# Each part of the folded weights loaded as two transfers, its blocks on SP's queue and its sums on ScalarE's

## The chip, the cores and the metric

The kernel runs on one core of a Trainium2 chip. The metric is the device time of one execution, in microseconds (us), as the median of several executions. The core's engines are named as in the profile: PE (TensorE; PEld is its weight load), DVE (VectorE), ACT (ScalarE), POOL (GpSimd) and SP (SyncE, which here only issues transfers). A transfer (DMA) is issued by SP or by ACT, in the order of that engine's own instructions.

## The reference

An attention without softmax is followed by a multiplicative feed-forward block, all in float32:

```python
kv  = einsum('bhsd,bhse->bhde', k, v)          # 8 batches, 8 heads, 576 tokens, head size 64
o   = einsum('bhsd,bhde->bhse', q, kv)
x   = o / sqrt(mean(o*o, axis=-1) + 1e-6) * g_norm     # then (B,H,S,D) -> (4608, 512)
out = ((x @ w1) * (x @ w2)) @ w3 @ w_out       # w1, w2: 512x1024, w3: 1024x1024, w_out: 1024x512
```

## The kernel before, in words

**Folding.** The product `w3 @ w_out` (1024 x 512, called `w3o`) is worked out once, in the first 85 us, and kept in `w3o_sb`. Each token then needs two stages: the gates, (x w1)(x w2), and the projection by `w3o`.

**Groups.** The 4608 tokens are worked on in nine groups T of 512. Eight groups are the first 512 tokens of a batch; group 8 collects the last 64 of all eight batches. The order is 0 to 6, 8, 7. While PE works on a group, the attention of the next batch is done in pieces that a callback, `between`, lets in between two products (lines 1110 to 1115).

**Gates.** `gates` (line 748) runs `winograd` (line 616) four times a group (p = 0 to 3): seven products instead of eight, each of 8 PE instructions, all at line 623. Two PSUM banks, `r1` and `r2`, take several products one after the other; before the next product may go on in a bank, ACT copies the bank out (`keep`, line 636: p1, p5, u2, u3; and line 758 for c21). So PE waits for ACT when a copy is late. The last of the seven, `product("a22", "t4", r1)` at line 655, needs the copy u3.

**Projection.** Group 0 uses `winograd` again (`project`). From group 1 on, `project_twice` (line 865) applies the same scheme twice: seven `products(n)` of 28 PE instructions each, all at line 900. `products(n)` reads a part of `w3o`: 1024 columns of blocks (b11, b12, b21, b22) and 768 columns of sums of blocks (t1, t2, t4), 128 rows of 1792 float32, or 896 KB. In each `products`, the order is a11 b11, a12 b21, a22 t4, s1 t1, s2 t2, s4 b22, s3 t3: the first read of a sum is the third pair, after 8 of the 28 PE instructions.

**Where the parts are.** There are seven such parts, and they do not fit on the chip beside everything else. In group 1, the generator `prepare_b` (line 801) works out the sums part by part on DVE (lines 819 to 822) and stores each part to the DRAM tile `w3o_l2` in two stores on SP: the blocks at line 823, the sums at line 826. Parts 0, 3, 4 and 5 have their blocks in `w3o_sb`, parts 1, 2 and 6 in `w3o_sums` (tiles named `raw`). An eighth part holds 1024 columns of plain blocks for the very last product.

**Streaming.** `load_b` (line 832) brings the parts back, 56 loads in all, into three buffers in turn (`streams`): two are halves of `w3o_sb`, one is a `raw` tile, memory that the stores of `prepare_b` have read from. The first three loads are made in group 1's gates: load 0 as soon as the last step of `prepare_b` has been issued (the fourth call of `between`, at p = 1), loads 1 and 2 at the next call (p = 2, between the copies u2 and u3). From then on `project_twice` makes one load after each product, into the buffer that the product has just read; it is wanted two products later.

**Order.** SP, POOL and PE issue in the order of the program text (line 1013). DVE does so in `project_twice` and in the gates of p = 3 just before it. ACT, and DVE elsewhere, are put in order by the framework's planner before the run, by its own estimate of when each operation's inputs are there. Once the order is set, an engine waits at an instruction whose input is late, and everything behind it waits too. An ACT transfer stands in ACT's order like any other instruction.

Of the kernel before, what the change touches and what calls it, by code (L numbers as in the profile page):

```python
# [21 lines left out]
def kernel(  # L22
# [32 lines left out]
    nc = tc.nc  # L55
# [634 lines left out]
    PART = 7 * 2 * P  # L690
# [139 lines left out]
    ALL_B = 7 * (NG - 1)  # L830

    def load_b():
        n = len(loaded_b)
        if n == ALL_B:
            return
        t = streams[n % len(streams)]

        part = {ALL_B - 2: 6, ALL_B - 1: 7}.get(n, n % 7)

        queue = nc.scalar if n % 7 in (3, 5) else nc.sync  # L840
        if n + 1 < ALL_B:
            queue.dma_start(out=t, in_=w3o_l2[part])
        else:
            t = t[:, 0:1024]
            queue.dma_start(out=t, in_=w3o_l2[part, :, 0:1024])
        loaded_b.append(t)

    inner = {}
# [16 lines left out]
    def project_twice(T, last, ahead):  # L865
# [94 lines left out]
        r1 = products(0)  # L960
        p1 = keep("p1", r1)
        load_b()
        sum_inner(2)
        for f in ahead:
            f()
        r2 = products(1)
        p5 = keep("p5", r2)
        load_b()
        sum_inner(3)
        products(2, r1)  # L970
        z = keep("u2", r1)
        load_b()
        sum_inner(4)
        products(3, r2)
# [35 lines left out]
    w3o_l2 = dram.tile([8, P, PART], FP32, name="w3o_l2")  # L1010
# [9 lines left out]
    with tc.manual_schedule(  # L1020
# [6 lines left out]
        for e in range(2):  # L1027
            nc.scalar.dma_start(
                out=g_row[:, e * D:(e + 1) * D], in_=g_norm.rearrange("(o d) -> o d", o=1)
# [156 lines left out]
```

## Time and profile before

| what | us |
|---|---|
| median of 6 executions | 768.95 |
| lowest and highest of them | 767.5, 770.59 |
| the profiled execution | 770.52 |
| its span, first to last instruction | 768.7 |
| PE busy in the span | 760.2 (99%) |
| DVE, ACT, POOL busy | 541.2, 253.7, 134.8 |

The profiled execution is 1.57 us slower than the median, and 1.8 us of it lie outside the span. In the profile, an engine's "idle before" says how long it stood still before an instruction and what ended that; a line such as `SPq L842` is SP issuing the transfer written at line 842. Issues of transfers are not counted as busy time of the engine that issues them, so ACT's 253.7 us leave them out. Times within the span are counted from its start.

The 56 loads appear as four rows of issues at line 842 and one at line 845: 39 of 896 KB on SP, 16 of 896 KB on ACT, and one of 512 KB on SP.

### The profile page before, as it was taken

The numbers are of one execution on the slowest core, as the hardware profiler recorded it, in microseconds if no ns is written. First come the engines' busy times: TensorE is split into PE (matmuls) and PEld (weight loads), VectorE is DVE, ScalarE is ACT, GpSimd is POOL, SyncE is SP. The second block draws the span as 40 slices with busy tenths as digits, with TensorE's granted clock in tenths as the row PEclk, the third lists the DMA queues.
The fourth block names the chain that finished last, engine by engine and source line by source line (L and its number), as shares of the span: only waits on it lengthen the run. The fifth ranks groups of instructions, "written<-read, shape, count | busy, mean of one in ns | idle before, by whom it ended". The sixth has DMA issues, their size and how long they took to land.

```text
span 768.7 us, 14426 instructions
## 1 busy us (share of the span) xinstructions
PE 760.2 (99%) x5775; PEld 660.2 (86%) x5775; DVE 541.2 (70%) x1083; ACT 253.7 (33%) x487; POOL 134.8 (18%) x132
## 2 busy tenths in 40 slices
PE   8999999999999999999999999999999999999998
PEld 6455788888899889988998899889888998898897
DVE  7977999438978577756776777557665864595467
ACT  6777753213322332223213321332133222222221
POOL 0000000122610451133114411340144000000000
PEclk9999999999999999999999999999999999999999
DMA  9996641338997844874487648734841470075015
GB/s 310 345 335 175 218 137 43 83 91 257 329 295 255 229 109 123 271 211 104 130 270 190 125 134 279 191 102 136 285 80 43 143 249 0 1 240 151 1 37 190
DMA packets 133159, 132.55 MB, mean 172 GB/s; under 512 B 76644, under 2 KB 121188, under 8 KB 133092
## 3 DMA queue, kind: packets, MB, share of 16 engines
q1 hardware_dynamic: 130640, 116.81, 51.8%
q10 hardware_dynamic: 2452, 14.81, 5.6%
q8 instruction: 46, 0.75, 0.4%
q14 instruction: 21, 0.17, 0.1%
HBM read 100.27 MB, written 16.38 MB: 152 GB/s over the span
## 4 chain that ended last, share of the span: by engine, by line
PE 94%; DMA 3%; DVE 2%; ACT 0%; issue 0%; SPq 0%; ACTq 0%; DVEq 0%
PE mm L623 60%; PE mm L900 19%; PE mm L602 7%; PE at L332 3%; PE at L415 2%; DMA raw<-in_moe_w_out_dram 1%; DMA w3o_sb<-w3o_l 1%; DMA raw<-w3o_l 1%; PE at L589 1%; PE at L351 1%; PE at L951 0%; DMA raw<-in_moe_w_dram 0%; PE at L448 0%; PE at L433 0%; DVE xc L666 0%; DVE raw L860 0%
## 5 line engine op out<-in xcount | busy, mean ns | idle before, releaser
L623 PE MATMUL mm<-xT,w_sb 128*128 128x256 f32 x768 | 176.2, 379 | 0.0
L623 PEld LDWEIGHTS mm<-xT,w_sb 128*128 128x128 f32 x768 | 145.5, 190 | 20.0 <-issue 0.5
L623 PE MATMUL mm<-xc,ws 128*128 128x256 f32 x576 | 130.3, 379 | 0.0
L623 PEld LDWEIGHTS mm<-xc,ws 128*128 128x128 f32 x576 | 109.3, 190 | 15.1 <-ACT p L636 0.2
L762 DVE TENSOR_TENSOR c<-mm,u 128x512 f32<-128x512 f32 x36 | 24.9, 690 | 108.3 <-PE mm L623 108.3
L636 ACT COPY u<-mm 128x512 f32<-128x512 f32 x74 | 43.3, 585 | 138.7 <-PE mm L623 128.0
L636 ACT COPY p<-mm 128x512 f32<-128x512 f32 x74 | 43.4, 586 | 84.1 <-PE mm L623 79.9
L623 PE MATMUL mm<-xc,w_sb 128*128 128x256 f32 x288 | 69.2, 383 | 0.0
L900 PE MATMUL mm<-w3o_sb,raw 128*128 128x128 f32 x500 | 62.5, 276 | 0.1
L602 PE MATMUL mm<-chunks,ab 128*128 128x512 f32 x128 | 60.2, 601 | 1.6 <-DVE chunks L170 0.8
L623 PE MATMUL mm<-xT,ws 128*128 128x256 f32 x256 | 61.2, 382 | 0.0
L763 DVE TENSOR_TENSOR ab<-c 128x256 f32<-128x256 f32 x108 | 59.0, 546 | 3.0
L290 POOL COPY xT<-xn 128x1024 uint16<-128x1024 uint16 x26 | 32.1, 1262 | 163.0 <-DVE xn L393 162.9
L623 PEld LDWEIGHTS mm<-xc,w_sb 128*128 128x128 f32 x288 | 53.7, 190 | 7.6
L900 PEld LDWEIGHTS mm<-w3o_sb,raw 128*128 128x128 f32 x500 | 59.0, 192 | 0.5 <-DVE raw L858 0.3
L623 PEld LDWEIGHTS mm<-xT,ws 128*128 128x128 f32 x256 | 47.9, 190 | 6.9 <-ACT p L636 0.3
L384 DVE TENSOR_REDUCE inv<-sq 128x8 f32<-128x512 f32 (+1 forms) x40 | 23.4, 626 | 36.4 <-ACT sq L383 36.4
L762 DVE TENSOR_TENSOR c<-p,u 128x512 f32<-128x512 f32 x36 | 28.2, 784 | 27.0 <-ACT u L636 26.9
L900 PE MATMUL mm<-w3o_sb,ab 128*128 128x128 f32 x336 | 43.9, 275 | 0.7 <-DMA w3o_sb<-w3o_l 0.7
L911 ACT COPY u<-mm 128x512 f32<-128x512 f32 x23 | 13.5, 586 | 87.6 <-DVE raw L924 60.3
L900 PEld LDWEIGHTS mm<-w3o_sb,ab 128*128 128x128 f32 x336 | 41.1, 192 | 1.2 <-issue 0.9
L602 PEld LDWEIGHTS mm<-chunks,ab 128*128 128x128 f32 x128 | 21.8, 190 | 22.6 <-issue 15.8
(158 smaller groups left out, 1138.4 us busy)
## 6 DMA issues: line engine op xcount, KB each, us to landing
w3o_sb<-w3o_l SPq DMA_DIRECT2D x26, 896.0 KB, 5.2
raw<-in_moe_w_dram SPq DMA_DIRECT2D x31, 512.0 KB, 7.2
raw<-w3o_l SPq DMA_DIRECT2D x13, 896.0 KB, 5.9
w3o_sb<-w3o_l ACTq DMA_DIRECT2D x11, 896.0 KB, 4.6
k_sb<-in_k_dram SPq DMA_DIRECT2D x32, 256.0 KB, 4.4
v_sb<-in_v_dram SPq DMA_DIRECT2D x32, 256.0 KB, 4.6
q_sb<-in_q_dram SPq DMA_DIRECT2D x32, 256.0 KB, 4.1
out_dram<-raw SPq DMA_DIRECT2D x14, 512.0 KB, 3.6
```

The source lines that it names most:

```text
L290: nc.gpsimd.tensor_copy(to, src.rearrange("p a n w -> p w a n"))
L332: nc.tensor.matmul(kv_ps[e * D:(e + 1) * D, r - rs[0], :], lhsT=k_sb[:, e, cols] if j < J else kl[:, 2 * r + e, :], rhs=v_sb[:, e, cols] i ...
L351: nc.tensor.transpose(qt_ps[:, e, i, :], q_sb[:, e, i * P:(i + 1) * P], ident)
L384: nc.vector.tensor_reduce(out=inv[:, i], in_=sq.rearrange("p (h d) -> p h d", d=D), axis=AX.X, op=ALU.add)
L415: nc.tensor.matmul(o_ps[l][tokens, n * D:(n + 1) * D], lhsT=qT[r][rows, e, i, tokens], rhs=kv_b[rows, e, r, :], start=True, stop=True,)
L602: nc.tensor.matmul(sums_ps[half][m], lhsT=w3T[half, c][:, m, :], rhs=chunks[:, c, 1, :], start=(c == 0), stop=(c == KF - 1),)
L623: nc.tensor.matmul(ps[:, u, :], lhsT=lhsT(a_name, u, c), rhs=rhs(b_name, c),  start=(u == 0 and c == 0 and to is None), stop=(c == chunks ...
L636: nc.scalar.copy(t, ps)
L762: nc.vector.tensor_add(c, one, two)
L763: nc.vector.tensor_mul(dst, c[:, 0, :], c[:, 1, :])
L900: nc.tensor.matmul(to[:, i, :], lhsT=x[:, c, :], rhs=y[:, c, :], start=new and place // 4 not in seen, stop=(c == 1), skip_group_check=True,)
L911: nc.scalar.copy(t[:, 0:4], ps[0])
```

## The change

Each load of a part becomes two transfers: the 1024 columns of blocks (512 KB) on SP's queue and the 768 columns of sums (384 KB) on ACT's queue. Until now a load was one transfer, on ACT's queue for loads 3 and 5 of every seven and on SP's queue for the others. The last load, of the eighth part, stays one transfer of 512 KB on SP's queue. The number of bytes, the buffers and the places of the calls of `load_b` are the same.

```diff
         part = {ALL_B - 2: 6, ALL_B - 1: 7}.get(n, n % 7)
 
-        queue = nc.scalar if n % 7 in (3, 5) else nc.sync
-        if n + 1 < ALL_B:
-            queue.dma_start(out=t, in_=w3o_l2[part])
-        else:
-            t = t[:, 0:1024]
-            queue.dma_start(out=t, in_=w3o_l2[part, :, 0:1024])
+        nc.sync.dma_start(out=t[:, 0:1024], in_=w3o_l2[part, :, 0:1024])
+        if part < 7:
+            nc.scalar.dma_start(out=t[:, 1024:PART], in_=w3o_l2[part, :, 1024:PART])
         loaded_b.append(t)
```

## The prediction

> **What bounds the kernel now.** I read the busy times first, then PE's rows in the projection stages, then the transfers, then ACT, SP and DVE in group 1.
>
> ```profile
> PE 760.2 (99%) x5775; PEld 660.2 (86%) x5775; DVE 541.2 (70%) x1083; ACT 253.7 (33%) x487; POOL 134.8 (18%) x132
> ```
>
> PE is busy for 99% of the span, so nothing can gain much; the question is where PE still stands still. The loads are read only in the projection stages. One of 196 instructions takes from its first L900 row to the first L623 row of the next group:
>
> ```profile
> 601.56 1.50 PE L900 MATMUL mm<-raw,ab 128*128 128x128 f32 x12
> ...
> 623.44 1.89 PE L623 MATMUL mm<-x_left,w_sb 128*128 128x256 f32 x8
> ```
>
> That is 21.88 us, or 0.112 per instruction and 3.13 per product. The stages that begin at 298.50, 373.95 and 450.21 take 21.88 too. Three take longer: 221.52 to 244.12 (22.60), 525.65 to 548.49 (22.84), 671.79 to 694.56 (22.77). The last two each hold one wait for a load:
>
> ```profile
> 545.29 1.57 PE L900 MATMUL mm<-w3o_sb,ab 128*128 128x128 f32 x12 [0.72 <-DMA w3o_sb<-w3o_l]
> 688.23 1.58 PE L900 MATMUL mm<-raw,ab 128*128 128x128 f32 x12 [0.65 <-DMA raw<-w3o_l]
> ```
>
> So late loads cost 0.96 + 0.89 = 1.85 us in this execution, and group 1's stage another 0.72, where PE waits for sums made by DVE (the chain of waits runs through DVE from 218 to 232.7). The whole that could be won from the loads is 1.85, with group 1's 2.57.
>
> **The transfers.** Issues at line 842 and 845, columns: how many, size, median us from issue to landing:
>
> ```profile
> w3o_sb<-w3o_l SPq DMA_DIRECT2D x26, 896.0 KB, 5.2
> w3o_sb<-w3o_l ACTq DMA_DIRECT2D x11, 896.0 KB, 4.6
> w3o_sb<-w3o_l SPq DMA_DIRECT2D x1, 512.0 KB, 3.5
> ```
>
> A load issued when product k has ended is wanted when k + 2 has: 2 x 3.13 less 0.2 for the issue, about 6.0 us. The medians fit in that; the two late ones landed after 6.8 and 6.7 us.
>
> **The change, part by part.**
>
> *Bytes and landing.* The two single-transfer rows, 512 KB in 3.5 and 896 KB in 4.6, give 1.1 us per 384 KB and so 2.0 us that do not depend on size. If the two halves of a load overlap, both land by about 4.6 as now; if one runs wholly after the other and pays the 2.0 again, the blocks land at 3.5 and the sums at 6.6. The sums are wanted 8 x 0.112 = 0.9 us after the blocks, at 6.9, so even then neither is late by itself. A load delayed by 2.2 us, as the two late ones were (6.8 against 4.6), would have blocks at 5.7 to 6.8: PE waits 0 to 0.8 instead of 0.9. I take a third of the 1.85 off, 0.6; the ends are 1.85 off and, if two more of the 32 urgent loads (four in each of eight stages) came late at 0.9 each, 1.8 on.
>
> The Trainium skill, page "DMA: Bandwidth & Descriptors", section "Rules for kernel authors", speaks against the split: issuing from several engines brings no bandwidth, since all share the same 16 DMA engines, and only saves issue time; it wants transfers of 1 MiB or more. Its fit of 2.0 us plus bytes / 436e3 (measured on another issuing path) would make 896 KB 4.1 us and the halves, one after the other, 6.1; by that the term would be the same.
>
> *Issues on SP.* 56 instead of 40, 16 more at 0.33 us (the L842 rows). They stand at loads 3 and 5 of a stage, where SP has nothing else: in the stage of 298.50 its last issue before ended at 292.6. In group 1 load 3 now comes behind SP's transposes, which end at 224.8; on ACT it went at 225.06. Nothing. The stores of results and the q, k, v loads behind load 9 are behind it already.
>
> *Issues on ACT.* 55 instead of 16, 39 more at 0.33, 12.8 us beside ACT's 33%. In the stages each stands after a product that has ended, or just before: for load 4 after p5's copy, 6 after product 3, when ACT's next row waits 6.60 us anyway; 7 after u3's copy, 8 after product 5, with ACT idle until 319.25 in that stage. Load 9 stands beside the last copy, and may push it by 0.33; the copy's results go to DVE, which then still has 1.5 us of rows of `finish(p1)` before it. Nothing in the stages; the end above is 0.33 for each of seven, 2.3.
>
> *PE's extra waits.* 55, one for each sums transfer. L900 has 82 such semaphore instructions of 51 ns now, nine of them in the stage at 298.50, which still takes 196 x 0.112. So 0; the end is 55 x 0.051 = 2.8.
>
> *The end of the program.* Load 54, 896 KB on ACT, becomes two; load 55 stays. Its product began without a wait; 0.
>
> *Group 1: three new waits in ACT's order.* Loads 0 to 2 were on SP alone. Their sums now stand in ACT's order, and they overwrite what the stores of `prepare_b` read. SP in group 1:
>
> ```profile
> 201.09 0.53 SPq L823 DMA_DIRECT2D w3o_l<-w3o_sb  x1
> 201.72 0.45 SPq L826 DMA_DIRECT2D w3o_l<-raw  x1
> 202.26 1.02 SPq L823 DMA_DIRECT2D w3o_l<-w3o_sb  x1
> 203.37 1.03 SPq L826 DMA_DIRECT2D w3o_l<-raw  x1
> 204.50 1.12 SPq L823 DMA_DIRECT2D w3o_l<-raw  x1
> 205.72 1.28 SPq L826 DMA_DIRECT2D w3o_l<-raw  x1
> 207.09 1.00 SPq L842 DMA_DIRECT2D w3o_sb<-w3o_l  x1
> ```
>
> The three L823 rows are the blocks of parts 4, 5 and 6. Asked one by one, they landed after 3.2, 6.2 and 6.1 us: at 204.3, 208.5 and 210.6. Load 0's sums lie over blocks of parts 0 and 4, load 1's over parts 3 and 5, load 2's over part 6. So ACT can issue them at 204.3, 208.5 and 210.6, and, if the issue also waits for the store of 205.72, about 211.9. ACT's rows there:
>
> ```profile
> 200.17 0.59 ACT L636 COPY u<-mm 128x512 f32<-128x512 f32 x1 [1.29 <-PE mm L623]
> ...
> 204.49 0.31 ACT L388 ACTIVATE inv<-inv,eps_col 128x16 f32<-128x16 f32 x1 [0.86 <-DVE inv L384]
> 206.22 0.58 ACT L636 COPY u<-mm 128x512 f32<-128x512 f32 x1 [1.43 <-PE mm L623]
> 209.63 0.37 ACT L758 COPY c<-mm 128x256 f32<-128x256 f32 x1 [2.82 <-PE mm L623]
> 211.36 0.58 ACT L636 COPY p<-mm 128x512 f32<-128x512 f32 x1 [1.35 <-PE mm L623]
> ```
>
> The row of 206.22 is u3, and PE's product a22 t4 begins at 207.70 and needs it: 0.9 us of slack after the copy's end at 206.80. In the text loads 1 and 2 stand before u3. If the planner leaves load 1's sums there, ACT waits until 208.5 or 211.9, issues (0.33; SP's issues took 1.0 in this crowd), copies u3 (0.58), and PE goes on at 209.4 to 213.5 instead of 207.70: 1.7 to 5.8 us lost. If it puts them after u3, c21 and p1 are late instead; p1's copy (0.58) has one product of 1.73 us (207.70 to 209.43) to hide beside, 1.1 of slack, and PE loses 0 to 0.9. What the order will be, no row shows. Two rows bear on it: the planner's order has been early before, with DVE held at L819 for a store's landing while a multiplication stood ready behind it:
>
> ```profile
> 185.10 0.43 DVE L819 TENSOR_TENSOR raw<-raw 128x256 f32<-128x256 f32 x1 [0.69 <-DMA w3o_l<-raw]
> 185.44 0.42 DVE L759 TENSOR_TENSOR ab<-c,mm 128x256 f32<-128x256 f32 x1
> ```
>
> and the stores from 202.26 on were slow in the run (issues of 1.0 us, landings of 6.2 against 3.2), which an order made beforehand is likelier to miss than to know. It need only expect load 1's turn 2.3 us before its time (206.2 for 208.5). I hold that a little likelier than not, and take 3.0, between the ends, nearer the direct one (2.0).
>
> *Sum.* +3.0 - 0.6 = +2.4. The profiled execution would go from 770.52 to 772.9; against the median, 768.95 + 2.4 = 771.4. That the median is 1.57 below the profiled execution says that other executions may have fewer late loads; the 0.6 is small for that reason too.
>
> **The rivals.**
>
> *ACT is not held before a copy that PE needs.* For it: DVE's subtractions for parts 3, 5 and 6 (L819 at 188.08, 198.98 and 200.66), which need earlier stores landed, met no wait, so the planner's times were good there. Then -0.6 and 0 to 0.9: 768.4 to 769.5, say 768.8, no change. It decides if load 1's sums stand after the row of 206.22.
>
> *The late loads go (the other side).* Blocks land ahead of sums, and PE never waits: -1.85, with group 1's DVE chain relieved -2.57: 767.1, or 766.4. It needs more than 1.54 us (0.2% of 768.95, about what a measurement of this kernel can tell from no change), so both late loads of an execution like the profiled one, and no stall in group 1. Against it: the lowest of the six executions is 767.5.
>
> *ACT is held from load 0 on.* In the text its sums stand before the copy of 194.84; held until 204.3 there, and again until 211.9 for load 1, ACT costs PE some 8 us: 776 to 778. Against it: the planner's orders follow readiness, not the text.
>
> *The split does nothing.* 40 issues move queues and all lands as before: 769, part of the first rival.
>
> **How the numbers follow.** Held before u3: 0.48 (770.0 to 774.5 by its ends). Not held: 0.33. Late loads gone: 0.13. Held from load 0: 0.06. Slower by over 0.2% is the first and the last, less a little for a stall of only 1.7 with relief: 0.52. Within 0.2%: 0.34. Faster: 0.14. The range leaves out half of the faster case and the case from load 0 on: 767.2 to 774.5.
>
> **What would show it.** In the changed kernel's ACT rows between 200 and 213, an issue at line 842's successor before the copy u3, u3 starting at 209 to 213, and PE's product after it idle 2 to 6 us, released by ACT. The other stages at 21.88, with fewer or shorter waits for loads. Wrong: u3 at its old place, or stages longer than 21.9 all through, which would be loads landing late or ACT's issues in the way.

## The result and the profile after

The changed kernel took 772.05 us (median of 22 executions, 770.97 to 775.59). The kernel before, run beside it, took 769.88 us (44 executions, 767.5 to 772.63). The ratio is 1.0031, with a 95% interval of 1.0021 to 1.0040: a little slower, by 2.4 us as the ratio has it (the two medians lie 2.2 apart). The differences of the experiments below go by their ratios too. The forecast was +2.4 us, from 768.95 to 771.4; the kernel before lies 0.9 above that 768.95 here, with 44 executions (the six among them).

The profiled execution took 771.1 us, with a span of 769.3. First the busy times and two groups of PE's rows, from the page of the changed kernel. In the groups, the columns after the bar are busy us and mean ns of one, and after the second bar the idle time just before the rows and what ended most of it. The product of `project_twice` is now at line 897, the blocks' transfer at 840, the sums' at 842.

```profile
PE 760.5 (99%) x5775; PEld 660.3 (86%) x5775; DVE 541.0 (70%) x1083; ACT 254.2 (33%) x487; POOL 135.3 (18%) x132
...
L623 PE MATMUL mm<-xc,w_sb 128*128 128x256 f32 x288 | 69.4, 384 | 1.8 <-ACT u L636 1.8
...
L897 PE MATMUL mm<-w3o_sb,raw 128*128 128x128 f32 x500 | 62.3, 275 | 0.6 <-DVE raw L856 0.6
```

PE is as busy as before. What is new is 1.8 us of idle time that a copy of ACT ended, and 0.6 us that DVE ended. No row of the projection waits for a load any more. The wait for ACT stands in group 1's gates. PE there (start, us, line, count, idle time before):

```profile
203.91 3.62 PE L623 MATMUL mm<-xT,w_sb 128*128 128x256 f32 x16
209.30 1.99 PE L623 MATMUL mm<-xc,w_sb 128*128 128x256 f32 x8 [1.77 <-ACT u L636]
211.13 1.89 PE L623 MATMUL mm<-xT,w_sb 128*128 128x256 f32 x8
```

In the kernel before, the same instructions:

```profile
204.25 3.62 PE L623 MATMUL mm<-xT,w_sb 128*128 128x256 f32 x16
207.70 1.89 PE L623 MATMUL mm<-xc,w_sb 128*128 128x256 f32 x8
```

There the eight of a22 t4 began 3.45 us after the 16 before them; in the changed kernel it is 5.39 us. So PE lost 1.93 us. And ACT, changed kernel, in the same stretch:

```profile
199.84 0.59 ACT L636 COPY u<-mm 128x512 f32<-128x512 f32 x1 [1.19 <-PE mm L623]
...
204.00 0.38 ACTq L842 DMA_DIRECT2D w3o_sb<-w3o_l  x1
204.43 1.09 ACT L383 ACTIVATE sq<-at 128x512 f32<-128x512 f32 x2 [2.25 <-PE mm L623]
208.06 0.36 ACTq L842 DMA_DIRECT2D w3o_sb<-w3o_l  x1
208.46 0.31 ACT L388 ACTIVATE inv<-inv,eps_col 128x16 f32<-128x16 f32 x1 [2.95 <-issue]
208.68 0.57 ACT L636 COPY u<-mm 128x512 f32<-128x512 f32 x1
211.71 0.40 ACTq L842 DMA_DIRECT2D raw<-w3o_l  x1
212.15 0.37 ACT L758 COPY c<-mm 128x256 f32<-128x256 f32 x1 [2.90 <-DMA w3o_l<-raw]
213.09 0.59 ACT L636 COPY p<-mm 128x512 f32<-128x512 f32 x1 [0.57 <-PE mm L623]
```

Look at the order. The sums of load 1 (208.06) stand ahead of `inv` and of u3 (208.68, before the change 206.22). They overwrite what the store of part 5's blocks reads, and that store landed at 208.00. Its issue on SP:

```profile
201.86 1.02 SPq L823 DMA_DIRECT2D w3o_l<-w3o_sb  x1
```

ACT stood at the transfer from 205.52 to 208.06, and what stands behind it had to wait. The row of `inv` names no releaser ("issue"); the run with load 1 alone, below, names the store.

The times between PE's starts, subtracted, account for the span. "To the first gates" is up to the first row of line 623, "to group 1's projection" from there to the first projection row.

| stretch | before, us | after, us | difference |
|---|---|---|---|
| to the first gates | 84.60 | 84.41 | -0.20 |
| to group 1's projection | 136.91 | 138.81 | +1.89 |
| group 1's projection | 22.61 | 23.44 | +0.83 |
| projection from 525.65 (before), one late load | 22.84 | 21.89 | -0.95 |
| projection from 671.79 (before), one late load | 22.77 | 21.88 | -0.89 |
| after the last projection | 7.08 | 6.96 | -0.12 |
| sum | | | +0.57 |

The other projections took the same in both kernels, 21.88 for those of 196 instructions. In the stage that had held the wait of 545.29, PE's rows now stand close (two of them, changed kernel, where a row of 16 is one unbroken stretch):

```profile
545.16 1.50 PE L897 MATMUL mm<-w3o_sb,inner_sums 128*128 128x128 f32 x12
546.50 1.95 PE L897 MATMUL mm<-w3o_sb,ab 128*128 128x128 f32 x16
```

The +0.83 in group 1's projection comes from DVE, which has there to make the sums that PE multiplies. DVE, changed kernel:

```profile
223.29 1.25 DVE L855 TENSOR_TENSOR raw<-ab 128x256 f32<-128x256 f32 x1
224.58 1.25 DVE L856 TENSOR_TENSOR raw<-raw,ab 128x256 f32<-128x256 f32 x1
225.86 0.42 DVE L857 TENSOR_TENSOR raw<-ab,raw 128x256 f32<-128x256 f32 x1
```

and POOL beside it, changed kernel:

```profile
222.88 2.68 POOL L304 COPY xT<-xn 128x1024 uint16<-128x1024 uint16 x2 [7.42 <-DMA xn<-xT]
```

PE, changed kernel, waiting for these sums:

```profile
225.88 1.17 PE L897 MATMUL mm<-w3o_sb,raw 128*128 128x128 f32 x8 [0.57 <-DVE raw L856]
227.35 0.71 PE L897 MATMUL mm<-w3o_sb,ab 128*128 128x128 f32 x4 [0.30 <-DVE ab L859]
```

Two rows of DVE took 1.25 us where such a row takes 0.42, and both lie beside POOL's two copies. Before, two rows took 1.26 and 1.37 beside the same copies, but the copies ran from 224.34, and the rows were later ones that PE did not want yet. The copies wait for the transposes of `xT` through SP. These began 2.35 us later than before (214.76 for 212.41) and were all issued 0.98 us earlier (220.69 for 221.67), while PE came 1.69 us later into the stage (223.21 for 221.52). So copies and urgent sums met. The run with the first three loads split, below, shows the same: copies from 224.40, DVE rows of 1.26 and 1.36 us from 224.56 and 225.75, and PE waiting for the sum behind them.

The issues of loads, changed kernel: count, size, median us from issue to landing:

```profile
w3o_sb<-w3o_l SPq DMA_DIRECT2D x38, 512.0 KB, 4.5
...
w3o_sb<-w3o_l ACTq DMA_DIRECT2D x37, 384.0 KB, 3.7
...
raw<-w3o_l SPq DMA_DIRECT2D x18, 512.0 KB, 4.8
...
raw<-w3o_l ACTq DMA_DIRECT2D x18, 384.0 KB, 4.4
```

By the medians, the halves land in less time than the whole did into `w3o_sb` (5.2 on SP, 4.6 on ACT), so on the whole one does not wait for the other.

### The profile page after: what moved, and what is told of

Read it like the earlier page. It is cut to its first block, busy times and chain, and to the rows that moved or that the text cites. A ratio compares the mean times of both kernels' runs of the same rounds, so it can differ in the third digit from the quotient of the medians.

```text
span 769.3 us, 14535 instructions
## 1 busy us (share of the span) xinstructions
PE 760.5 (99%) x5775; PEld 660.3 (86%) x5775; DVE 541.0 (70%) x1083; ACT 254.2 (33%) x487; POOL 135.3 (18%) x132
## 4 chain that ended last, share of the span: by engine, by line
PE 91%; DVE 3%; DMA 3%; SPq 1%; ACT 1%; issue 1%; ACTq 0%; DVEq 0%
PE mm L623 55%; PE mm L897 22%; PE mm L602 7%; PE at L332 2%; PE at L415 2%; DMA raw<-in_moe_w_out_dram 1%; DMA w3o_l<-raw 1%; PE at L589 1%; SPq L294 1%; PE at L351 1%; DVE c L762 1%; DMA w3o_l<-w3o_sb 0%; PE at L948 0%; DMA raw<-in_moe_w_dram 0%; DMA out_dram<-raw 0%
## 5 line engine op out<-in xcount | busy, mean ns | idle before, releaser
L762 DVE TENSOR_TENSOR c<-p,u 128x512 f32<-128x512 f32 x36 | 26.3, 731 | 26.4 <-ACT u L636 26.3
```

The costliest lines, as they stand in the source:

```text
L762: nc.vector.tensor_add(c, one, two)
```

## The experiments

The theory: ACT holds load 1's sums before u3, and this costs the time. The rivals for the cause: the split itself costs time in the stages (two transfers for one, 39 more issues on ACT), or the crowd of transfers in group 1 does. Four ran beside a kernel before of 769.27 us (23 executions), three beside one of 769.17 (29).

### The first three loads whole, the others split

```diff
-        nc.sync.dma_start(out=t[:, 0:1024], in_=w3o_l2[part, :, 0:1024])
-        if part < 7:
-            nc.scalar.dma_start(out=t[:, 1024:PART], in_=w3o_l2[part, :, 1024:PART])
+        if n < 3:
+            nc.sync.dma_start(out=t, in_=w3o_l2[part])
+        else:
+            nc.sync.dma_start(out=t[:, 0:1024], in_=w3o_l2[part, :, 0:1024])
+            if part < 7:
+                nc.scalar.dma_start(out=t[:, 1024:PART], in_=w3o_l2[part, :, 1024:PART])
```

> Loads 0 to 2 stay whole on SP, the other 53 are split. Theory (the loss is ACT held by the sums of loads 0 to 2 in group 1): no hold, so PE's product after u3 begins without a wait, the stages at 21.9 us, and the time is that of before less what late loads cost, -0.3 to -1.0 us. Rival (the split itself costs in the stages: more transfers, ACT's issues between its copies): +2.0 us or more, spread over the eight stages.

It took 769.03 us, ratio 0.9998 (0.9989 to 1.0008). ACT's u3 is back at its old place:

```profile
206.43 0.59 ACT L636 COPY u<-mm 128x512 f32<-128x512 f32 x1 [1.43 <-PE mm L623]
```

PE's product after it began 3.45 us after the 16 instructions before it (204.46 and 207.91), the projections took 21.88, and none waited for a load. So 52 loads split this way cost nothing (by the interval 0.6 us at most), and the loss lies in the first three. The gain of 0.2 us is a little under the expected 0.3 to 1.0.

### Only the first three loads split

```diff
+        if n < 3:
...
+        else:
...
```

Under `if` stand the two transfers of the change, under `else` the code of before.

> Only loads 0 to 2 are split, the rest as before. Theory: ACT is held as in the changed kernel, PE loses 1.9 us before u3 and up to 0.8 more in group 1's stage; late loads stay as before: +2.3 to +3.0 us. Rival (the split in the stages costs): 0 to +0.3 us.

It took 773.0 us, ratio 1.0050 (1.0033 to 1.0067), so +3.8, with +2.5 as the interval's lower end. The loss is there without the other splits. PE's rows:

```profile
204.06 3.62 PE L623 MATMUL mm<-xT,w_sb 128*128 128x256 f32 x16
209.65 1.99 PE L623 MATMUL mm<-xc,w_sb 128*128 128x256 f32 x8 [1.98 <-ACT u L636]
```

The wait for u3 is 2.14 us by the starts. Group 1's projection took 23.58 us, with PE waiting 1.41 for a sum of DVE. The loss came out above the expected 2.3 to 3.0. Two of the six executions have a mean granted clock of 0.997, of which more below; the median of the other four is 772.2, or +2.9. With six executions the size is only roughly known.

### Only load 1 split

```diff
+        if n == 1:
+            nc.sync.dma_start(out=t[:, 0:1024], in_=w3o_l2[part, :, 0:1024])
+            if part < 7:
+                nc.scalar.dma_start(out=t[:, 1024:PART], in_=w3o_l2[part, :, 1024:PART])
+        else:
...
```

Under `else` stands the code of before.

> Only load 1 is split, all else as before. Theory: its sums alone hold ACT before u3 until the store of part 5 has landed, PE loses 1.5 to 2.2 us there, and the total is +1.5 to +2.5 us. Rival (it takes all three holds, or the crowd of transfers in group 1): under +0.7 us.

It took 772.63 us, ratio 1.0038 (1.0023 to 1.0053): +2.9, above the expected 1.5 to 2.5, though the interval reaches into it. One transfer of 384 KB, out of 56 loads, brings the whole loss. ACT:

```profile
208.07 0.36 ACTq L843 DMA_DIRECT2D w3o_sb<-w3o_l  x1
208.55 0.59 ACT L636 COPY u<-mm 128x512 f32<-128x512 f32 x1 [4.57 <-DMA w3o_l<-w3o_sb]
```

Here the trace names the releaser: u3 came 4.57 us after ACT's row before it, and what ended the wait is the landing of the store out of `w3o_sb`. PE, same kernel:

```profile
203.44 3.62 PE L623 MATMUL mm<-xT,w_sb 128*128 128x256 f32 x16
209.19 2.49 PE L623 MATMUL mm<-xc,w_sb 128*128 128x256 f32 x8 [2.14 <-ACT u L636]
211.47 3.12 PE L623 MATMUL mm<-xT,w_sb 128*128 128x256 f32 x8
214.43 2.75 PE L623 MATMUL mm<-xc,ws 128*128 128x256 f32 x12
```

PE lost 2.30 us in the wait, and then more: the eight instructions of 211.47 took 3.12 us, where such a row takes 1.89. Its window (columns: us; busy time and count of PE, weight loads, DVE, ACT, POOL; granted clock; share of the DMA engines; GB/s):

```profile
211.00:214.30 3.30, 3.30 (x10) 2.63 (x9) 3.13 (x8) 0.37 (x1) 0.15 (x1) 0.55 0.95 343
```

and the same window of the changed kernel's profiled execution:

```profile
211.00:214.30 3.30, 3.30 (x17) 2.91 (x16) 3.16 (x5) 0.96 (x2) 3.30 (x4) 1.00 0.98 344
```

The granted clock was 0.55 in the one and 1.00 in the other. From 209.19 to 214.43 the 16 instructions took 5.24 us, for 3.45 at full clock, so that this cost 1.8 us more. The other five executions have a mean clock of 1.0 and a median of 772.58, so the lowered clock is not what makes the +2.9.

### Loads 0 and 2 split, load 1 whole

```diff
+        if n in (0, 2):
...
+        else:
...
```

Under `if` stand the two transfers of the change, under `else` the code of before.

> Loads 0 and 2 are split, load 1 and the rest as before: the counterpart to the run with load 1 alone. Theory (only a hold before u3 costs): ACT is held before sq and before c21, PE not or by under 0.6 us: 0 to +0.9 us. Rival (each hold costs its share): +1 to +2 us.

It took 770.17 us, ratio 1.0015 (1.0000 to 1.0030), +1.15. ACT:

```profile
204.41 0.37 ACTq L843 DMA_DIRECT2D w3o_sb<-w3o_l  x1
...
207.44 0.58 ACT L636 COPY u<-mm 128x512 f32<-128x512 f32 x1 [0.37 <-DVE c L762]
212.19 0.37 ACTq L843 DMA_DIRECT2D raw<-w3o_l  x1
212.60 0.37 ACT L758 COPY c<-mm 128x256 f32<-128x256 f32 x1 [4.57 <-DMA w3o_l<-raw]
```

Without load 1's sums u3 is 1.2 us late instead of 2.5, and PE waits only 0.21 us for it and 0.14 for p1. The long wait for load 2's sums (4.57 us) cost almost nothing, since c21 and p1 had room. So load 1 carries nearly all of the wait, by its place in the order. The time alone does not say so: +1.15 is above what was expected (0 to 0.9) and within the rival's +1 to +2, and its interval reaches from no loss to 2.3. What speaks for it is the profile, with 0.21 and 0.14 us at these two places. It has four further PE waits of 0.75 to 0.76: one in group 1's projection and three far from it, one of these for a load.

### The changed kernel with load 0 to 2's sums behind u3

Here all 55 transfers stay on ACT. Only the place of three of them in ACT's order is changed: ACT follows the text in these gates, and the sums stand one or two calls of `between` later.

```diff
-        if part < 7:
+        def sums_too():
             nc.scalar.dma_start(out=t[:, 1024:PART], in_=w3o_l2[part, :, 1024:PART])
+        if n < 3:
+            owed.append(sums_too)
+        elif part < 7:
+            sums_too()
...
+                calls.append(0)
+                for f in {6: owed[0:2], 7: owed[2:3]}.get(len(calls), []):
+                    f()
...
-            gates(T, p, between if T or p else lambda: None)
+            if (T, p) == (1, 2):
+                with tc.manual_schedule(engines={mybir.EngineType.Activation}):
+                    gates(T, p, between)
+            else:
+                gates(T, p, between if T or p else lambda: None)
```

> The changed kernel with every transfer kept, 55 on ACT; only the sums of loads 0 to 2 stand behind the copy u3 in ACT's order (two behind it by the text, ACT in the order of the text in the gates of group 1, p = 2). Theory: u3 is at its old place, the 1.9 us before PE's next product are gone; c21 and p1 behind the transfers are late instead, 0 to 0.9 us: -0.6 to +0.8 us against before, 1.5 us or more below the changed kernel. Rival (the crowd of transfers in group 1, or ACT's 39 more issues, make the loss): as the changed kernel, +2 us.

It took 768.43 us, ratio 0.9989 (0.9974 to 1.0004). ACT:

```profile
206.03 0.58 ACT L636 COPY u<-mm 128x512 f32<-128x512 f32 x1 [1.43 <-PE mm L623]
206.18 2.59 ACTq L843 DMA_DIRECT2D w3o_sb<-w3o_l  x2
210.57 0.39 ACTq L843 DMA_DIRECT2D raw<-w3o_l  x1
211.00 0.37 ACT L758 COPY c<-mm 128x256 f32<-128x256 f32 x1 [4.38 <-DMA w3o_sb<-w3o_l]
```

u3 goes first, and ACT then waits for the same stores: those of the blocks of parts 5 and 6 landed at 208.39 and 210.54, and ACT issued at 208.41 and 210.57. PE has no gap there: a22 t4 began 3.45 us after the row before it. ACT's other rows in this stretch stand in the order of the kernel before. The same transfers on the same queues, three of them placed later, and the loss is gone; the time is even just below the expected range. This is the run that shows the order in ACT as the cause.

### Both halves on SP

```diff
-            nc.scalar.dma_start(out=t[:, 1024:PART], in_=w3o_l2[part, :, 1024:PART])
+            nc.sync.dma_start(out=t[:, 1024:PART], in_=w3o_l2[part, :, 1024:PART])
```

> Every load split as in the changed kernel, both transfers on SP. Theory: without a transfer in ACT's order nothing holds ACT; the waits for the stores fall to SP: no stall before u3, and -0.8 to +0.3 us against before. Rival (two transfers instead of one cost by themselves, by packets and landings): about as slow as the changed kernel, +2 us.

It took 768.45 us, ratio 0.9993 (0.9984 to 1.0002); u3 at 206.57. With ACT out of it, the split costs nothing. A second queue brings nothing either, as far as these runs can tell.

### Both halves on SP, sums first

```diff
-        nc.sync.dma_start(out=t[:, 0:1024], in_=w3o_l2[part, :, 0:1024])
         if part < 7:
-            nc.scalar.dma_start(out=t[:, 1024:PART], in_=w3o_l2[part, :, 1024:PART])
+            nc.sync.dma_start(out=t[:, 1024:PART], in_=w3o_l2[part, :, 1024:PART])
+        nc.sync.dma_start(out=t[:, 0:1024], in_=w3o_l2[part, :, 0:1024])
```

> Every load split, both transfers on SP, the sums ahead of the blocks. PE reads a buffer's sums for the last time two pairs (8 instructions, 0.9 us) before its blocks, so the sums can go that much earlier. Theory: no hold of ACT, fewer late loads than before: -1.0 to 0 us against before. Rival (SP, now waiting for two things a load, delays what stands behind it, or the blocks behind the sums land late): +0.5 us or more.

It took 768.27 us, ratio 0.9989 (0.9979 to 0.9998), 0.9 us below the kernel before and some 0.4% below the changed one. It is the best of the kernels here, though by little. Its 0.9 us and those of the two before it lie too close together to say what the order of the halves is worth.

## Why the prediction came right, point by point

**Group 1's waits in ACT's order, +3.0.** The mechanism is the one that was named, at the place that was named: load 1's sums before u3, held by a store of `prepare_b`, and PE's a22 t4 late by it. By its ends, 1.7 to 5.8, the truth was near the lower one: 1.93 in the profiled execution, 2.14 and 2.30 in the two experiments. The sums waited for the blocks' store of part 5 (predicted landing 208.5, measured 208.00), not for the last store, which landed at 212.21. The signs that were named, u3 at 209 to 213 and PE idle for 2 to 6 us, were just missed at their lower ends (208.68 and 1.93). The 3.0 was on the high side for the wait itself. But two things that the sum did not have came behind it: a lowered clock in part of the executions, and the +0.83 in group 1's projection. The median of the 15 executions without a lowered clock is 771.58. So it is in part luck that the total came out so near: a wait taken too long stood in for two terms that were missing. Load 1 alone cost +2.9 over all. Two figures of the working do not fit its own terms: 768.95 + 5.8 - 0.6 gives 774.2 for the upper end, where it has 774.5, and the direct wait that it calls 2.0 comes to 1.7 by its own terms, as at its lower end.

**Loads 0 and 2.** Load 0's sums were predicted at 204.3 and went at 204.00. Load 2's were predicted at 210.6, or 211.9 with the last store, and went at 211.71, when the blocks' store of part 6 had landed (211.69), which took 7.6 us instead of 6.1. With u3 late, PE had no wait for p1; with loads 0 and 2 alone it was 0.14, at the low end of the 0 to 0.9 that were predicted.

**Bytes and landing, -0.6.** In the profiled execution both late loads went, -1.85, more than the third that was taken. Of all profiled executions here, five with the loads from 3 on split have no wait of this kind, and four with them whole have two, none, one and one. That is one execution of each. The times are the better measure: the split without ACT's wait brings 0.2 us (52 loads split) to 0.9 (the sums behind u3, and both on SP with the sums first), and only the last of them has an interval wholly below 1. So 0.6 lies within what was measured, which is too small to size it better, and the rival "late loads go", with 1.85, was too large; by the four profiles, not every execution has two late loads to lose.

The Trainium skill, page "DMA: Bandwidth & Descriptors", section "Rules for kernel authors", had been quoted against a gain from a second queue. Both halves on SP took 768.45 and halves on two queues (with the wait mended) 768.43, which agrees.

**Issues and PE's waits, 0.** Right: from group 2 on, every projection of 196 instructions without a wait for a load took 21.88 us, in all kernels. The 55 further semaphore instructions of PE did not come: the line of the product has 86 of them in the changed kernel, for 82 before. The places of the issues were partly wrong, too. For load 4 the sums were put after p5's copy, and it stands between the two copies of such a pair of rows (changed kernel, ACT):

```profile
306.15 0.59 ACT L908 COPY p<-mm 128x512 f32<-128x512 f32 x1 [1.31 <-PE mm L897]
306.59 0.33 ACTq L842 DMA_DIRECT2D raw<-w3o_l  x1
307.49 0.48 ACT L909 COPY p<-mm 128x384 f32<-128x384 f32 x1 [0.75 <-PE mm L897]
```

The blocks of that load left SP only at 307.48. In a product the last read of the 768 columns is s2 t2, and two more pairs, s4 b22 and s3 t3, read the 1024 columns (t3 lies among those). Two pairs are 8 instructions of 0.112 us, so as a transfer of their own the sums start 0.9 us earlier. The prediction gave the sums 0.9 us of room at the other end, and had not seen this.

**Group 1's projection.** The prediction gave it nothing against the change, and a gain in one rival. It lost 0.83 in the profiled execution. This is the term that was missed. Its cause was read from rows of DVE and POOL, and no run here tested it alone, so it is argued and not shown. It is 22.28 to 22.74 us in the kernels where u3 is on time, or nearly (before 22.61), and 22.87, 23.44 and 23.58 where u3 is late.

**The rivals.** "Not held" is what the mended order does, at 768.43 for the 768.8 that were worked out. "Held from load 0 on", 776 to 778, did not come: the planner put load 0's sums behind the copies of `kv_sb`, and ACT stood there only from 202.18 to 204.00, when their store had landed (203.91). That hold fell before `sq`; by the run with loads 0 and 2 it makes u3 1.2 us late and costs PE 0.21.

**The base.** The sum stood on a profiled execution 1.57 above the median of six. It went up by only 0.6 in the profile, as its two late loads were lost in the bargain, while the medians differ by 2.2. The forecast against the median was the better for taking a small share of the 1.85.

## What to carry to other kernels

A transfer that is put on an engine's queue is an instruction of that engine: look first at what it has to wait for (here a store that still reads the buffer), and then at what stands behind it and how much slack that has. One such transfer of 384 KB before one copy cost 2.9 us here, while 52 others on the same queue cost nothing. On SP, which only issues transfers here, the same split cost nothing (768.45 for 769.27).

## What the runs showed of the hardware

**PE's clock after a short gap.** In the run with only load 1 split, a stretch of 2.30 us before 209.19 has 0.16 us of PE work in it, and PE's clock record stands at half from 210.55 on, for 3.41 us. Where PE lost 1.93 and 2.14 us, the profiled executions (the changed kernel, and the first three loads split) kept their clock. The mean granted clock, 0.997 in that run's execution, tells how often it happens: of the changed kernel's 22 executions, seven have 0.997 or 0.998, and these took 772.59 to 775.59 us (median 773.61), against a median of 771.58 for the other 15. In the three kernels with u3 held by load 1's sums, ten of 34 executions have such a mean; in the other five and the 52 executions of the kernel before that ran beside the experiments, ten of 110. So a lowered clock was found more often with the gap, and also without it; that the gap caused it is likely by these counts, and not shown. The Trainium skill, page "TensorE: Matmul & The Clock Gate", section "🔬 Part 1: The HAM clock gate (the "warmup" mystery)", says that the clock is halved after at least one idle window of some 3.4 us, free-running at 3413 ns. The length of the lowered stretch agrees; the gap before it is shorter than a window.

**DVE beside POOL.** A DVE row of 0.42 us took 1.25 to 1.37 beside a copy of POOL, in both kernels. The Trainium skill, page "SBUF — State Buffer", section "Who interferes with whom", says that a `tensor_tensor` with both inputs in that memory contends with reads of GpSimd (POOL), calls the ports that they share an exclusive lock, and says that the order of issue decides who is blocked. The rows agree: the first of POOL's two copies ended at 224.27 and the second at 225.55, DVE's two long rows, each begun during one of them, at 224.54 and 225.83.

**SP waits for transfers of ACT.** In the changed kernel SP stood still in group 1 for landings (waits of SP from 205 to 223 us; columns: us in total, times, longest):

```profile
SPq L840 <- DMA w3o_sb<-w3o_l: 1.7, 1, 1.7
...
SPq L294 <- DMA raw<-w3o_l: 1.0, 1, 1.0
SPq L95 <- DMA w3o_sb<-w3o_l: 0.9, 1, 0.9
```

Before, SP had no wait for a landing there. Two of these three ended when sums on ACT's queue landed, load 0's at 210.46 (line 95) and load 2's at 218.43 (line 294). The one at line 95 is a load of `v`, which shares no buffer with `w3o_sb`. Why it waited for a load of `w3o` stays open. No row of PE waited for what SP had behind it.
